# Decode attention on one core: keys loaded one pair ahead of values, and the loads of the first and the last pairs cut differently

## The chip, the cores and the metric

One core of one Trainium2 chip runs the kernel. The metric is the time of one execution in device microseconds, as a median of several runs. Engines, as the profile names them: PE multiplies matrices (PEld is the loading of its stationary operand), DVE is the vector engine, ACT the scalar engine, POOL the GpSimd engine, SP the engine that issues nearly all loads. An engine works through its own instructions in order; engines wait for each other through semaphores.

## The reference

```python
B, Hq, Hkv, Sq, Sk, D = 1, 32, 8, 1, 65536, 128      # q, k, v in bfloat16
rep = Hq // Hkv
k = jnp.repeat(k, rep, axis=1)
v = jnp.repeat(v, rep, axis=1)
scale = D ** -0.5
scores = jnp.einsum("bhqd,bhkd->bhqk", q, k) * scale
p = _softmax(scores, axis=-1)
return jnp.einsum("bhqk,bhkd->bhqd", p, v)
```

One new token attends to 65,536 cached positions. Four query heads share each of eight key and value heads. Keys and values are 134.2 MB each, 268.4 MB together, and every byte is used once.

## The kernel before

The sequence of one key head is cut into four chunks of 128 x 128 positions. Two chunks are a *pair*, so a head has two pairs and the program 16 (`NP`); a pair's keys are 8.4 MB and its values 8.4 MB. `n` is the chunk in the pair. A chunk is 128 tiles of 128 positions, worked on in 16 units of 8 tiles (`j`).

**Keys.** A unit's eight tiles are transposed by PE against an identity (line 135), copied from PSUM to SBUF by DVE (line 207) or, for j = 3, 7, 11, 15, by ACT (line 205), and then multiplied with the head's four queries (line 144); the scores follow the transposes three units later. **Softmax.** For each chunk DVE takes the maximum (line 225), POOL takes it across partitions (line 393), DVE merges it with the old one, ACT makes the exponentials (line 347) and the factor alpha (line 351) by which DVE rescales the sum and the output so far. **Values.** PE multiplies the 128 exponentials' tiles with the value tiles into PSUM (line 162), and DVE adds the result to `acc` (lines 257, 259, 309). In the last pair the old `acc` goes into the last chunk's accumulation through an fp32 matmul with the identity (line 155).

**Loops.** PE runs a loop over the 16 pairs: keys of both chunks, then values of both chunks. ACT loops over pairs, DVE and POOL over heads with two pairs in the body. SP's code (lines 413 to 448) is written out pair by pair.

**Buffers and loads.** `kbuf` holds a whole pair of keys (two halves), `bbuf` one chunk, `vbuf` a whole pair of values. For pairs 1 to 13 (`WHOLE`) the keys come in one load into `kbuf`; POOL (six copies, line 213) and ACT (two, line 356) copy the second half into `bbuf`, from which PE reads chunk 1. For the other pairs chunk 1 is loaded into `bbuf` directly. SP issues in the order K0 V0 K1 V1 ... K15 V15. Three semaphores hold it: `kfree`, three times a pair (POOL's copies done, ACT's copies done, chunk 0's last transposes done), for the next keys; `bfree` (chunk 1's last transposes done) where `bbuf` is loaded directly; `vfree` (DVE has seen the end of the pair's values) for the next values. A load that is cut into pieces has a semaphore for each piece, which PE awaits at the piece's first tile; where a pair comes whole, SP raises the other pieces' semaphores itself (`tokens`). `K_PIECES` and `V_PIECES` are the sizes of the pieces in tiles; `pieces` are used for pair 0's keys, pair 15's first chunk of keys and pair 15's values.

Of the kernel before, what the change touches and what calls it, by code (L numbers as in the profile page):

```python
# [25 lines left out]
K_PIECES = ((64, 64), (64, 64))  # L26
V_PIECES = ((128,), (73, 38, 13, 4))
# [10 lines left out]
def on_act(j):  # L38
    return j % 4 == 3
# [12 lines left out]
def bass_standalone__gqa_softmax__decode_kernel(nc, q, k, v, out):  # L52
# [32 lines left out]
    cmax = sb("cmax", [P, R], DT.float32)  # L85
# [5 lines left out]
    rsum = sb("rsum", [P, R], DT.float32)  # L91
# [17 lines left out]
    vp = [[sem(f"vp{i}_{p}") for p in range(len(V_PIECES[i]))] for i in range(2)]  # L109

# [6 lines left out]
    acr, l_sem, lws = sem("acr"), sem("l_sem"), sem("lws")  # L117
    xd, xa, xg = sem("xd"), sem("xa"), sem("xg")
# [19 lines left out]
    def pe_scores(pe, n, j):  # L138
        take(pe, eva if on_act(j) else evd)
        if n == 0 and j == 0:  # L140
            take(pe, qrdy)
# [7 lines left out]
    def pe_values(pe, n, lap):  # L149
        vv = vbuf[:, n * T * D:(n + 1) * T * D].rearrange("p (t d) -> p t d", d=D)  # L150
        for t in range(T):
            if n and t == V_PIECES[1][0]:
                with pe.If(lap == NP - 1):
                    pe.wait_ge(acr, H)
                    pe.matmul(pvb[n][:, 0:R], lhsT=identf[:, :], rhs=acc[:, :], start=False, stop=False)  # L155
            if t == 0:
                take(pe, vp[n][0], 16)
                take(pe, exd)
            piece = vp[n][starts(V_PIECES[n]).index(t)] if t and t in starts(V_PIECES[n]) else None
            if piece:  # L160
                pe.wait_ge(piece, 16)
            ins = pe.matmul(pvb[n][:, 0:R], lhsT=vv[:, t, :], rhs=pts[n][:, t * R:(t + 1) * R],  # L162
                            start=t == 0, stop=t == T - 1)
            if piece:
                pe.sem_inc(piece, -16)
        ins.then_inc(pvd, 1)

    def pe_pair(pe, lap):
# [9 lines left out]
        for n in range(2):  # L178
            pe_values(pe, n, lap)

    def tensor_engine(pe):
# [6 lines left out]
        with pe.Fori(0, NP) as lap:  # L188
            pe_pair(pe, lap)
        pe.wait_ge(t_f, H)  # L190
# [33 lines left out]
    def chunk_max(e, n):  # L224
        e.tensor_reduce(cmax[:, :], qkb[n][:, :].rearrange("p (t g) -> p g t", g=R),  # L225
                        AX.X, ALU.max).then_inc(cm, 1)

    def new_max(e, n, fresh):
        take(e, cma)

        mn, mo = m[n], m[1 - n]
# [30 lines left out]
    def dve_pair(e, second, lap):  # L262

        fresh, last = not second, second
        for j in range(G):
            if not on_act(j):
                evict(e, 0, j)
# [218 lines left out]
```

## Time and profile before

| what | us |
|---|---|
| median of 3 runs | 628.18 (628.08 to 628.23) |
| span of the profiled execution, first to last instruction | 626.94 |
| what lies around it (median less span) | 1.24 |

No time of the profiled execution itself is listed beside its span; the median of the runs stands for it. In timelines a row gives start, duration, engine, line, operation and the tiles written and read; brackets give the idle time of the engine before it and what ended it. `SPq` rows are loads issued by SP. "issue" as a releaser means that the profile shows nothing that the engine waited for. In the list of loads the last number is the time from issue to landing.

### The profile page before, as it was taken

Reading aid. Unit: us, or ns where it says so; the run is one execution under the profiler, and the core shown is the slowest. Engines: PE = TensorE matmul, PEld = TensorE weight load, DVE = VectorE, ACT = ScalarE, POOL = GpSimd, SP = SyncE. Lnnn points to the kernel's source line nnn. Section 1 sums busy time; section 2 is a strip of 40 time slices with the busy share of each in tenths; the row PEclk is TensorE's granted clock in tenths of the full one; section 3 lists DMA queues with packets and bytes.
Section 4 is the critical chain, followed back from the end, with each engine's and each line's share of the span. In section 5 each row is a group of like instructions: output and inputs, shape, how many; then the busy total and the mean of one; then the engine's idle time right before and its main releaser. Section 6 shows DMA issues by size and latency. Waiting matters only on the chain. (4 is left out here: it accounts for less than half of the span.)

```text
span 626.9 us, 27931 instructions
## 1 busy us (share of the span) xinstructions
PE 484.6 (77%) x12340; PEld 478.9 (76%) x12340; DVE 315.1 (50%) x699; ACT 228.9 (37%) x445; POOL 159.9 (26%) x124
## 2 busy tenths in 40 slices
PE   5752995959859498694976959679496894999698
PEld 5752995949859498694976959679496894999698
DVE  4620752817537174371734717356183562848274
ACT  2320532615335153341634407245062441624133
POOL 0000704307042070520605115060150702400000
PEclk9965875958769587695966959678596785969597
DMA  8999999999999999999999999999999999999997
GB/s 366 440 449 424 439 431 439 431 439 426 443 422 447 410 460 410 460 406 460 410 439 431 426 443 426 443 426 439 431 439 431 439 431 435 416 447 424 420 433 302
DMA packets 6280, 268.57 MB, mean 428 GB/s; under 512 B 896, under 2 KB 1024, under 8 KB 1152
## 3 DMA queue, kind: packets, MB, share of 16 engines
q1 hardware_dynamic: 6224, 268.45, 99.2%
q8 instruction: 6, 0.10, 0.1%
q10 hardware_dynamic: 48, 0.01, 0.0%
q14 instruction: 2, 0.02, 0.0%
HBM read 268.44 MB, written 0.01 MB: 428 GB/s over the span
## 5 line engine op out<-in xcount | busy, mean ns | idle before, releaser
L207 DVE COPY ktb<-trb 128x1024 bf16<-128x1024 bf16 x384 | 254.6, 689 | 177.5 <-PE trb L135 173.7
L205 ACT ACTIVATE ktb<-trb 128x1024 bf16<-128x1024 bf16 x128 | 131.0, 1023 | 352.7 <-PE trb L135 297.9
L135 PE MATMUL trb<-ident,kbuf 128*128 128x128 bf16 x2048 | 177.1, 245 | 104.7 <-PEq L49 104.6
L135 PEld LDWEIGHTS trb<-ident,kbuf 128*128 128x128 bf16 x2048 | 143.9, 111 | 105.6 <-issue 105.5
L213 POOL COPY bbuf<-kbuf 128x2048 bf16<-128x2048 bf16 x78 | 143.9, 1893 | 177.6 <-POOLq L49 177.6
L144 PE MATMUL qkb<-qcur,ktb 128*128 128x4 bf16 x4096 | 174.3, 165 | 11.8 <-PEq L49 10.3
L144 PEld LDWEIGHTS qkb<-qcur,ktb 128*128 128x128 bf16 x4096 | 155.2, 97 | 14.6 <-issue 14.6
L135 PE MATMUL trb<-ident,bbuf 128*128 128x128 bf16 x2048 | 157.0, 220 | 5.2 <-issue 3.9
L162 PE MATMUL pvb<-pts,vbuf 128*128 128x4 bf16 x4096 | 113.0, 166 | 15.2 <-PEq L49 11.0
L162 PEld LDWEIGHTS pvb<-pts,vbuf 128*128 128x128 bf16 x4096 | 111.1, 103 | 16.6 <-issue 15.6
L135 PEld LDWEIGHTS trb<-ident,bbuf 128*128 128x128 bf16 x2048 | 117.4, 97 | 5.5 <-issue 5.5
L393 POOL PARTITION_ALL_REDUCE cmaxa<-cmax x32 | 11.9, 370 | 254.1 <-POOLq L49 254.1
L347 ACT ACTIVATE pts<-qkb,negm 128x128 bf16<-128x128 f32 x128 | 50.9, 549 | 37.2 <-ACTq L49 37.2
L356 ACT ACTIVATE bbuf<-kbuf 128x2048 bf16<-128x2048 bf16 x26 | 49.5, 1902 | 0.0
L347 ACT ACTIVATION_READ_ACCUMULATOR pts<-qkb,negm 128x1 f32 x128 | 35.6, 278 | 0.0
L225 DVE TENSOR_REDUCE cmax<-qkb 128x4 f32<-128x512 f32 x32 | 22.0, 686 | 23.4 <-DVEq L49 23.4
L259 DVE TENSOR_TENSOR acc<-acc,pvb 128x4 f32<-128x4 f32 x16 | 2.5, 158 | 30.0 <-PE pvb L162 30.0
L257 DVE COPY acc<-pvb 128x4 f32<-128x4 f32 x8 | 1.3, 163 | 21.8 <-PE pvb L162 21.8
L395 POOL PARTITION_ALL_REDUCE la<-lp x8 | 3.4, 430 | 30.7 <-POOLq L49 30.7
L236 DVE SCALAR_TENSOR_TENSOR negm<-cmaxa,m 128x4 f32<-128x4 f32 x24 | 3.9, 163 | 11.7 <-DVEq L49 11.5
L351 ACT ACTIVATE alpha<-dm 128x4 f32<-128x4 f32 x32 | 7.1, 221 | 0.0
L250 DVE TENSOR_TENSOR acc<-acc,alpha 128x4 f32<-128x4 f32 x24 | 3.9, 164 | 6.1 <-DVEq L49 5.7
(44 smaller groups left out, 41.6 us busy)
## 6 DMA issues: line engine op xcount, KB each, us to landing
kbuf<-in_k_dram SPq DMA_DIRECT2D x4, 2048.0 KB, 16.3
bbuf<-in_k_dram SPq DMA_DIRECT2D x2, 4096.0 KB, 20.9
bbuf<-in_k_dram SPq DMA_DIRECT2D x2, 2048.0 KB, 19.9
kbuf<-in_k_dram SPq DMA_DIRECT2D x1, 4096.0 KB, 16.3
vbuf<-in_v_dram SPq DMA_DIRECT2D x1, 4096.0 KB, 21.9
vbuf<-in_v_dram SPq DMA_DIRECT2D x1, 2336.0 KB, 27.1
vbuf<-in_v_dram SPq DMA_DIRECT2D x1, 1216.0 KB, 29.6
vbuf<-in_v_dram SPq DMA_DIRECT2D x1, 416.0 KB, 30.1
```

The source lines that it names most:

```text
L135: ins = pe.transpose(trb[j % NTB][:, i * P:(i + 1) * P], kv[:, t, :], ident[:, :])
L144: ins = pe.matmul(qkb[n][:, t * R:(t + 1) * R], lhsT=ktb[:, off:off + P], rhs=qcur[:, :], start=True, stop=True)
L162: ins = pe.matmul(pvb[n][:, 0:R], lhsT=vv[:, t, :], rhs=pts[n][:, t * R:(t + 1) * R], start=t == 0, stop=t == T - 1)
L205: e.activation(dst, trb[j % NTB][:, :], AF.Copy).then_inc(eva, 1)
L207: e.tensor_copy(dst, trb[j % NTB][:, :]).then_inc(evd, 1)
L213: ins = op(bbuf[:, c * CB * D:(c + 1) * CB * D], kbuf[:, off:off + CB * D])
L225: e.tensor_reduce(cmax[:, :], qkb[n][:, :].rearrange("p (t g) -> p g t", g=R), AX.X, ALU.max).then_inc(cm, 1)
L236: return e.scalar_tensor_tensor(to[:, :], cmaxa[:, :], -scale, mo[:, :], ALU.mult, ALU.min)
L347: ins = e.activation(pv[:, g, :], sv[:, g, :], AF.Exp, bias=negm[:, g:g + 1], scale=scale, accum_out=rsum[:, g:g + 1])
L351: e.activation(alpha[:, :], dm[:, :], AF.Exp, scale=1.0).then_inc(sx, 1)
L356: return e.activation(o, i, AF.Copy)
L393: e.partition_all_reduce(cmaxa[:, :], cmax[:, :], P, bass.bass_isa.ReduceOp.max).then_inc(cma, 1)
```

## The change

- SP's order becomes K0 K1 V0 K2 V1 ... K15 V14 V15. `keys(p)` issues a pair's keys, for pairs 1 to 13 also waits for `bfree`, and `values(p - 1)` follows it.
- PE's loop has 17 laps: lap p does the keys of pair p, then the values of pair p - 1; the first lap skips the values and the last one the keys, by branches on the lap.
- The softmax step is done once for a pair instead of once for a chunk: both maxima and their maximum on DVE, one reduction on POOL, eight exponentials in a row and one alpha on ACT.
- The values of both chunks go into one PSUM accumulation, which starts with the fp32 identity matmul of `acc`; `acc` is zero for a head's first pair and the rescaled PSUM result for its second. DVE finishes a head's output in the next pair.
- Exponentials now wait until the previous pair's values have used their buffer (`pfree`), and PE's scores wait until the previous pair's exponentials have read the scores (`exd`).
- Pair 14's values come in two loads. Pair 15's values follow into the same buffer half by half: the first half when pair 14's first half has been used (`vhalf`, raised by ACT), the second after `vfree`.
- Pieces: chunk 0's keys of pairs 0 and 15 in 32, 40 and 56 tiles, their chunk 1 in one; the last chunk of values in 73, 33, 15 and 7.

```diff
-K_PIECES = ((64, 64), (64, 64))
-V_PIECES = ((128,), (73, 38, 13, 4))
+K_PIECES = ((32, 40, 56), (128,))
+V_PIECES = ((128,), (73, 33, 15, 7))
...
     def pe_scores(pe, n, j):
         take(pe, eva if on_act(j) else evd)
-        if n == 0 and j == 0:
-            take(pe, qrdy)
+        if j == 0:
+            take(pe, exd)
+            if n == 0:
+                take(pe, qrdy)
...
+    def pe_values(pe, lap):
+        take(pe, acr)
+        pe.matmul(pvb[0][:, 0:R], lhsT=identf[:, :], rhs=acc[:, :], start=True, stop=False)
+        for n in range(2):
+            vv = vbuf[:, n * T * D:(n + 1) * T * D].rearrange("p (t d) -> p t d", d=D)
+            sems = dict(zip(starts(V_PIECES[n]), vp[n]))
+            for t in range(T):
+                piece = sems.get(t)
+                if piece:
+                    pe.wait_ge(piece, 16)
+                ins = pe.matmul(pvb[0][:, 0:R], lhsT=vv[:, t, :], rhs=pts[n][:, t * R:(t + 1) * R],
+                                start=False, stop=n == 1 and t == T - 1)
+                if piece:
+                    pe.sem_inc(piece, -16)
+            ins.then_inc(pvd if n else pfree, 1)
...
-        with pe.Fori(0, NP) as lap:
-            pe_pair(pe, lap)
-        pe.wait_ge(t_f, H)
+        with pe.Fori(0, NP + 1) as lap:
+            with pe.If(lap < NP):
+                pe_keys(pe)
+            with pe.Else():
+                pe.wait_ge(exd, 2)
+            with pe.If(lap > 0):
+                pe_values(pe, lap)
+        pe.wait_ge(t_f, 1)
...
+    def pair_max(e):
+        for n in range(2):
+            take(e, qkd)
+            ins = e.tensor_reduce(cmax[:, n * R:(n + 1) * R], qkb[n][:, :].rearrange("p (t g) -> p g t", g=R),
+                                  AX.X, ALU.max)
+        own(e, ins, xd)
+        e.tensor_tensor(cmaxp[:, :], cmax[:, 0:R], cmax[:, R:2 * R], ALU.max).then_inc(cm, 1)
...
+        for n in range(2):
+            for j in range(G):
+                if not on_act(j):
+                    evict(e, n, j)
+                if n == 0 and j == 0:
+                    e.sem_inc(pgo, 1)
+        pair_max(e)
+        if second:
             next_queries(e)
         else:
             e.sem_inc(qrdy, 1)
-        values_done(e, 0, fresh)
-        rescale(e, 1, False)
...
+        new_max(e, second)
+        if second:
+            values_done(e)
+        else:
+            with e.If(lap > 0):
+                values_done(e)
+                own(e, e.tensor_tensor(oT[:, HR - R:HR], pvb[0][:, 0:R], recip[:, :], ALU.mult), xd)
...
+        take(e, sx)
+        if not second:
+            e.memset(acc[:, :], 0.0).then_inc(acr, 1)
...
+        e.tensor_tensor(acc[:, :], pvb[0][:, 0:R], alpha[:, :], ALU.mult).then_inc(acr, 1)
...
-        for j in (3, 7):
+        for j in (3, 7, 11, 15):
             evict(e, 1, j)
-        exps(e, 0)
-        for j in (11, 15):
-            evict(e, 1, j)
-        exps(e, 1)
+        for n in range(2):
+            take(e, pfree)
+            if n == 0:
+                e.sem_inc(vhalf, 1)
+            exps(e, n)
+        take(e, dmr)
+        e.activation(alpha[:, :], dm[:, :], AF.Exp, scale=1.0).then_inc(sx, 1)
...
+        def keys(p):
             if p:
                 e.wait_ge(kfree, 3 * p)
             if WHOLE[0] <= p < WHOLE[1]:
-                e.dma_start(kbuf[:, :], ks).then_inc(kp[0][0], 16)
+                e.dma_start(kbuf[:, :], src(kf, p)).then_inc(kp[0][0], 16)
                 tokens(kp[0][1:])
...
+                e.wait_ge(bfree, p)
+                tokens(kp[1])
+                return
+            key_unit(p, 0)
             if p:
+                e.wait_ge(bfree, p)
+            key_unit(p, 1)
...
+        def values(p):
+            vs = src(vf, p)
+            if p < NP - 2:
+                if p:
+                    e.wait_ge(vfree, p)
                 e.dma_start(vbuf[:, :], vs).then_inc(vp[0][0], 16)
...
+            for n in range(2):
+                if p == NP - 2:
+                    if not n:
+                        e.wait_ge(vfree, p)
+                    e.dma_start(half(vbuf, n), half(vs, n)).then_inc(vp[n][0], 16)
+                    tokens(vp[n][1:])
+                else:
+                    e.wait_ge(vfree if n else vhalf, p + 1 - n)
+                    pieces(half(vbuf, n), half(vs, n), V_PIECES[n], vp[n])
+
+        for p in range(NP):
+            keys(p)
+            if p:
+                values(p - 1)
+        values(NP - 1)
```

165 lines of the change are left out of this document (48 added, 117 removed).

## The prediction

> **What bounds the kernel now.** I read the page first, then the chain of waits, the loads with their issues, and the timeline of three stretches: pair 0, a steady pair, the tail.
>
> ```profile
> span 626.9 us, 27931 instructions
> PE 484.6 (77%) x12340; PEld 478.9 (76%) x12340; DVE 315.1 (50%) x699; ACT 228.9 (37%) x445; POOL 159.9 (26%) x124
> q1 hardware_dynamic: 6224, 268.45, 99.2%
> q8 instruction: 6, 0.10, 0.1%
> ```
>
> SP's queue keeps the 16 DMA engines busy for 99.2% of the span; the busiest compute engine has 77%. So the time is that of one unbroken stream of loads, plus a lead-in and a tail. An engine made faster is worth nothing; a load issued after its predecessor has drained costs exactly its lateness.
>
> ```profile
> 63.08 3.50 PE L135 MATMUL trb<-ident,kbuf 128*128 128x128 bf16 x32 [9.04 <-PEq L49]
> 64.40 11.07 POOL L213 COPY bbuf<-kbuf 128x2048 bf16<-128x2048 bf16 x6 [25.25 <-POOLq L49]
> ...
> 75.70 0.33 SPq L418 DMA_DIRECT2D kbuf<-in_k_dram  x1
> 333.99 3.57 PE L135 MATMUL trb<-ident,kbuf 128*128 128x128 bf16 x32 [7.96 <-PEq L49]
> 335.43 11.07 POOL L213 COPY bbuf<-kbuf 128x2048 bf16<-128x2048 bf16 x6 [10.83 <-POOLq L49]
> 346.73 0.33 SPq L418 DMA_DIRECT2D kbuf<-in_k_dram  x1
> 358.12 3.45 PE L162 MATMUL pvb<-pts,vbuf 128*128 128x4 bf16 x128
> 358.30 0.69 DVE L225 TENSOR_REDUCE cmax<-qkb 128x4 f32<-128x512 f32 x1 [1.37 <-DVEq L49]
> 361.38 0.21 ACT L351 ACTIVATE alpha<-dm 128x4 f32<-128x4 f32 x1
> 361.74 3.55 PE L162 MATMUL pvb<-pts,vbuf 128*128 128x4 bf16 x128 [0.17 <-PEq L49]
> ...
> 365.51 0.33 SPq L437 DMA_DIRECT2D vbuf<-in_v_dram  x1
> ```
>
> PE starts a pair when its keys land, after 8 to 9 us of idling. From pair 1 (63.08) to pair 8 (333.99) are 7 pairs in 270.91 us: 38.70 us a pair, 19.35 us for each 8.4 MB load. The keys of pair 1 are the third load in the row, so pair 0's keys had landed at 63.0 - 2 x 19.35 = 24.3. In a pair the next keys are issued 12.7 us after PE's start (333.99 to 346.73, set by POOL's copies), the values' matmuls begin at +24.1, and the next values are issued at +31.5.
>
> ```profile
> 592.83 2.23 SPq L407 DMA_DIRECT2D vbuf<-in_v_dram  x5
> 625.77 0.25 SPq L448 DMA_DIRECT2D out_dram<-lrow  x1
> vbuf<-in_v_dram SPq DMA_DIRECT2D x1, 4096.0 KB, 21.9
> vbuf<-in_v_dram SPq DMA_DIRECT2D x1, 2336.0 KB, 27.1
> vbuf<-in_v_dram SPq DMA_DIRECT2D x1, 128.0 KB, 29.9
> 620.83 0.04 issue
> 620.88 2.08 PE pvb L162 x73
> 622.96 0.43 PE pvb L155 x2
> 623.39 1.59 PE pvb L162 x55
> 625.00 0.17 DVE oT L305
> ```
>
> The five last loads are issued 0.45 us apart, so the 128 KB piece goes out at 594.6 and lands at 594.6 + 29.9 = 624.5. PE's last 130 instructions run back to back to 624.98: in the tail PE and the stream end together, within 0.5 us. The 1.96 us after that are output.
>
> **The change part by part.** *The stream.* Bytes stay. Loads go from 42 to 44: pair 0's keys stay four (3+1 for 2+2), pair 15's go from three to four, pair 14's values from one to two, pair 15's values stay five. The price of one more load: 2336 KB landed 5.6 us after the 4096 KB (592.83 + 21.9 = 614.7; 593.3 + 27.1 = 620.4, rounded by 0.1), where 2.39 MB at 8.39 MB per 19.35 us are 5.5. I take 0.08 each; two are **+0.15 us** (0 to 0.4).
>
> *The tail.* The fp32 matmul of the old accumulator (0.43) moves from the middle of the last 128 matmuls to their head, where PE waits for data. PE no longer has the keys and all values of the last load's time to do: after the last landing it has 7 matmuls left instead of 4, 3 x 0.029 = 0.09 us (29 ns from 55 in 1.59). Against PE's 0.5 us after the landing now, I take **-0.05** (-0.3 to +0.3).
>
> *DVE, ACT, POOL.* 16 maxima across partitions, alphas and rescalings disappear, 16 small combinations appear, all 0.16 to 0.4 us; PE gets 15 more fp32 matmul pairs, 0.43 each. In a pair this is +24.1 + 0.43 + 7.2 (358.12 to 365.29) = +31.9, and 6.8 us of the 38.7 stay idle. Cover: the stream. **0.**
>
> *The issues* are where it can lose. A wait on SP holds every later load, as SP issues all of them in order. A small DMA takes 625.77 to the span's end, 1.2 us, so I let every issue need 1.2 us before the queue runs dry:
>
> ```profile
> 8.18 3.57 PE L135 MATMUL trb<-ident,kbuf 128*128 128x128 bf16 x32 [2.94 <-PEq L49]
> 18.91 0.61 PE L135 MATMUL trb<-ident,kbuf 128*128 128x128 bf16 x8
> 19.68 0.33 SPq L418 DMA_DIRECT2D kbuf<-in_k_dram  x1
> 22.75 0.21 PEld L144 LDWEIGHTS qkb<-qcur,ktb 128*128 128x128 bf16 x6 [0.62 <-issue]
> 31.69 0.23 PEld L135 LDWEIGHTS trb<-ident,bbuf 128*128 128x128 bf16 x4 [4.04 <-issue]
> 37.40 0.34 PE L144 MATMUL qkb<-qcur,ktb 128*128 128x4 bf16 x8 [0.78 <-PEq L49]
> 51.02 2.93 PEld L162 LDWEIGHTS pvb<-pts,vbuf 128*128 128x128 bf16 x107 [3.11 <-issue]
> 605.28 0.61 PE L135 MATMUL trb<-ident,bbuf 128*128 128x128 bf16 x8 [1.36 <-PEq L49]
> 617.25 3.44 PE L162 MATMUL pvb<-pts,vbuf 128*128 128x4 bf16 x128
> ```
>
> - Keys of pair 1 now follow pair 0's directly, so they must be out by 24.3 - 1.2 = 23.1. Before, 64 tiles landed at 8.1 and the last transposes ended at 19.52. With 32 tiles first PE starts 32 x 0.076 = 2.4 us earlier, meets the third piece at 13.0, and ends near 17.6: issue at 17.8, cover 5 us.
> - Values of pair 0 wait for bfree, the last transposes of pair 0. Its second half is one piece now and lands at 24.3; 12.0 us of work (605.28 to 617.25), 1.5 for the slow start after idling (32 transposes in 3.57 where eight take 0.61), and 2 to 4 for the stop at 31.69. Keys end at E0 = 40 to 42, transposes 1.7 earlier; issued by 40.5, needed by 43.6 - 1.2. Cover 2 us.
> - Keys of pair 2 go out 12.6 us after pair 1's start (63.08 to 75.70); needed by 63.0 - 1.2 = 61.8. So pair 1 may start as late as 49.2, instead of 43.7. Keys' end to alpha's end is 3.5 us now (358.1 to 361.6); with the second maximum (0.7), the combining (0.3) and four more exponentials (1.4) it is 5.9, and only then DVE evicts again (1.0 us after a start, 63.1 to POOL's 64.4 less 0.3): start in effect at E0 + 4.9 = 45 to 47. Cover 2 to 4 us.
> - In steady pairs: keys 19.35 - 12.7 - 1.2 = 5.4 us of cover, values 38.7 - 32.1 - 1.2 = 5.4.
> - First half of pair 15's values waits until values 14, first half, are done. From the landing of the last keys: 12.0 + 0.43 + 3.45 + 0.3 for ACT and SP + 1.2 = 17.4, against 19.4 us that pair 14's values take. Cover 2 us. The second half: landing + 3.5 + 0.3 + 1.2 = 5.0 into the 9.7 us of the first.
>
> Everywhere there is cover, so the sum is 0.15 - 0.05 + 0 = **+0.1**: 627.0 of span. The runs lie 628.18 - 626.94 = 1.24 above the profiled span, so **628.3 us**.
>
> **The rivals.** *Code not yet loaded.* PE halted at 27.6 to 31.69 and at 47.9 to 51.02 for no semaphore, in lap 0 alone, and the page has just six instruction packets: PE runs into code still being fetched behind the loads. Now lap 0 ends with a jump over the 256 value matmuls (512 instructions with their weight loads), which have never run, to the loop's end. From the stop at 22.75, the first moment to ask for the code that came at 31.69, are 8.9 us; 3.1 is the shortest of the two long stops. So the jump costs 3.1 to 8.9, and pair 1 starts at E0 + 3 to 9 = 43.7 to 51. Past 49.2 the keys of pair 2 are late by the excess, 0 to 1.8 us; with a second fetch behind the first (the values' own code is asked for at the same time) 2 to 4. Price 2: **630.3**. For it: two stops seen in straight code. Against: no halt shows at the loop's back edge, and the jump's first 5 us lie under the wait for keys. The Trainium skill, page "Runtime: NRT & Kernel Launch", section "Instruction fetch mechanics", says that a taken branch to a block outside the loaded window forces a fetch of the target before execution continues; the two stops agree with fetching by blocks, and no trace here shows such a jump.
>
> *All the code again.* If that jump also throws out what was loaded, lap 1 stops at each of six blocks, 3 to 4 us each: keys 2 and values 1 late by 10 to 15 us, **640**. Against it: laps 1 to 15 of before never refetch.
>
> *The turn at pair 15.* If PE goes through keys 15 and values 14 at the slow pace (3.57 for 32 against 0.61 for eight, 1.46 times), the 12.0 become up to 17.5 and the first half goes out 3 us late: **631**. Against: the same stretch in before ran at 0.61 throughout.
>
> *A shorter end.* If the PE backlog held the end more than the 0.5 us that I read, or the lead-in shortens with the smaller first piece, at most 1.5 us: **627**. Against: pieces had landed at 624.5.
>
> **How the numbers follow.** Forecast 0.48, late keys of pair 2 0.32, the turn 0.07, all code again 0.07, shorter end 0.06. A difference under 0.2% (1.26 us) cannot be told from none: 629.4 and 626.9 are the limits. Of the late keys three quarters pass 629.4 (0.24), with the turn and the code 0.38 slower; shorter end gives 0.05 faster; 0.57 remains. The likeliest case's own range is 627.9 to 628.8. To leave out 0.2, the range goes down to 627.6 (tail at its lower bound, half the shorter end) and up to 632.0 (late keys with the second fetch; the turn).
>
> **What would show it.** Right: SP's queue at 99%, PE's wait at pair 1 within 43.7 to 49, the issue of pair 2's keys before 61.8, the last first-half issue of values 2 us before pair 14's values end, PE's end waiting for pieces. Wrong: DMA slices under 9 around 60 to 65 us (late keys), many more instruction packets (code again), a dip near 600 (the turn).

## The result and the profile after

The changed kernel takes **631.96 us** (median of 6 runs, 629.19 to 634.87) against 628.23 (628.08 to 628.33) measured beside it: a ratio of 1.0061, 95% interval 1.0039 to 1.0083. It is slower, by 3.7 us, and its runs scatter over 5.7 us where those of before scatter over 0.25. The forecast was 628.3; the time lies in the range, at its upper end.

The profiled run is one of 631.01 us with a span of 629.5, so 1.5 lie around it, 0.3 more than before; it is 0.95 us under the median. Its page:

```profile
span 629.5 us, 27800 instructions
...
DMA  9999999999999999999999999999999999999997
...
q1 hardware_dynamic: 6512, 268.45, 99.1%
q8 instruction: 6, 0.10, 0.1%
```

SP's queue is still the bound, at 99.1%, and no digit of the DMA row but the last is under 9: slices of 15.7 us are too wide to show a gap of 2. As many instruction packets run as before, so code is not fetched again. The timeline of PE at the turn from pair 0 to pair 1, and at pair 2 (start, duration, instructions; in brackets the idle time before and what ended it):

```profile
38.68 0.34 PE L149 MATMUL qkb<-qcur,ktb 128*128 128x4 bf16 x8 [0.68 <-PEq L49]
47.37 3.30 PE L138 MATMUL trb<-ident,kbuf 128*128 128x128 bf16 x32 [8.35 <-PEq L49]
...
84.47 3.51 PE L138 MATMUL trb<-ident,kbuf 128*128 128x128 bf16 x32 [6.46 <-PEq L49]
```

The one branch over the values' code, grouped by its source line (shortest, median and longest of 17 executions in ns, first and last start):

```profile
L193 PEldq COMPARE_BRANCH  x17: 76/76/7600, 39.0 to 613.0; - x17
```

In lap 0 the branch takes 7.60 us, in the others 0.08. It is the jump over code that has never run: from 39.0 to 46.6 PE's sequencer does nothing else. The Trainium skill, page "Runtime: NRT & Kernel Launch", section "Instruction fetch mechanics", has a taken branch outside the loaded window wait for a fetch; the 7.60 us agree with that. What follows from it stands in SP's issues and in the windows of the DMA share (after the busy times of PE, PEld, DVE, ACT and POOL, each with its count, come the granted clock, the share of the 16 engines and GB/s; a packet counts where it begins, so a full window can show more than 1):

```profile
37.54 0.33 SPq L433 DMA_DIRECT2D vbuf<-in_v_dram  x1
60.00 0.33 SPq L416 DMA_DIRECT2D kbuf<-in_k_dram  x1
78.19 0.33 SPq L433 DMA_DIRECT2D vbuf<-in_v_dram  x1
```

```profile
60.00:62.00 2.00, 2.00 (x57) 2.00 (x54) 1.44 (x3) 0.61 (x1) 0.00 (x0) 1.00 1.04 360
62.00:64.00 2.00, 2.00 (x57) 2.00 (x54) 1.97 (x3) 0.44 (x2) 0.00 (x0) 1.00 0.52 197
64.00:66.00 2.00, 2.00 (x55) 2.00 (x52) 1.40 (x4) 1.00 (x1) 0.00 (x0) 1.00 1.09 459
```

The keys of pair 2 are issued at 60.00, 12.6 us after PE's start at 47.37, as costed. In the window from 62 to 64 only half as many packets begin as the engines could take: the queue ran dry. To size it I read the trace's landing records (when the last of the 16 engines reports its share of a load): a load of 8.4 MB lands 19.35 us after the one before it as long as the queue is full, so what a period has over 19.35 (9.72 for half a load) is lost. Pair 0's values land at 63.03 and pair 2's keys at 84.33, 21.30 later: **1.95 us lost**. The other periods up to pair 14 are 19.35, most within 0.02 (one of 19.45 is followed by one of 19.26); only those of pair 1's keys (19.60) and pair 0's values (19.44) are longer for good, while instruction blocks pass through the same engines. The last piece lands at 627.03 instead of 624.56, 2.47 later: 1.95 from the hole and 0.5 from the lead-in and the smaller loads of pairs 14 and 15.

I call *lead* the time from an issue to the landing of the load in flight (here 63.03 - 60.00 = 3.03 us). The second thin place is at the end:

```profile
604.06 8.85 SPq L395 DMA_DIRECT2D vbuf<-in_v_dram  x5
```

```profile
578.00:584.00 6.00, 6.00 (x136) 6.00 (x134) 5.17 (x9) 2.05 (x2) 0.00 (x0) 0.89 1.00 431
...
604.00:606.00 2.00, 0.00 (x0) 0.00 (x0) 0.00 (x0) 1.59 (x8) 0.00 (x0) 0.50 0.97 311
606.00:608.00 2.00, 0.71 (x24) 0.71 (x25) 0.00 (x0) 0.00 (x0) 0.00 (x0) 0.50 0.65 279
```

Pair 15's first half of values goes out at 604.06 with 3.19 us of lead (pair 14 lands at 607.25). The share sinks to 0.65, but the landings keep their 9.72: the engines that ran ahead idled, the slowest did not (the 16 engines end pair 14 between 604.48 and 607.25).

### The profile page after: what moved, and what is told of

It reads as the page before. It is cut to its first block, busy times and chain, and to the rows that moved or that the text cites. A ratio compares the mean times of both kernels' runs of the same rounds, so it can differ in the third digit from the quotient of the medians.

```text
span 629.5 us, 27800 instructions
## 1 busy us (share of the span) xinstructions
PE 490.4 (78%) x12370; PEld 484.9 (77%) x12370; DVE 303.0 (48%) x601; ACT 230.5 (37%) x429; POOL 154.0 (24%) x108
## 3 DMA queue, kind: packets, MB, share of 16 engines
q1 hardware_dynamic: 6512, 268.45, 99.1%
## 5 line engine op out<-in xcount | busy, mean ns | idle before, releaser
L381 POOL PARTITION_ALL_REDUCE cmaxa<-cmaxp x16 | 5.9, 371 | 261.8 <-POOLq L49 261.8
L288 DVE TENSOR_TENSOR acc<-pvb,alpha 128x4 f32<-128x4 f32 x8 | 1.3, 162 | 58.4 <-DVEq L49 58.4
L279 DVE TENSOR_TENSOR oT<-pvb,recip 128x4 bf16<-128x4 f32 x7 | 1.1, 163 | 38.2 <-DVEq L258 38.2
L156 PE MATMUL pvb<-acc,identf 128*128 128x4 f32 x32 | 6.7, 280 | 4.9 <-PEq L49 4.9
L156 PEld LDWEIGHTS pvb<-acc,identf 128*128 128x128 f32 x32 | 5.8, 226 | 5.9 <-issue 5.9
L322 DVE TENSOR_TENSOR oT<-pvb,recip 128x4 bf16<-128x4 f32 x1 | 0.2, 162 | 12.7 <-PE pvb L164 12.7
## 6 DMA issues: line engine op xcount, KB each, us to landing
vbuf<-in_v_dram SPq DMA_DIRECT2D x1, 1056.0 KB, 13.6
```

The source lines that it names most:

```text
L156: pe.matmul(pvb[0][:, 0:R], lhsT=identf[:, :], rhs=acc[:, :], start=True, stop=False)
L381: e.partition_all_reduce(cmaxa[:, :], cmaxp[:, :], P, bass.bass_isa.ReduceOp.max).then_inc(cma, 1)
```

## The experiments

Theory A: the jump makes PE late for pair 1, so the keys of pair 2 are issued to a queue that is nearly dry. Rivals (theory B in the expectations): the pieces or the order of the loads cost by themselves; the fetching of instructions costs by itself; the turn at pair 15. Times are medians with the range of the runs; ratios are to the kernel before on the same chip.

**1. The changed kernel again, and the pieces alone.** The first without an edit; the second is the kernel before with

```diff
-K_PIECES = ((64, 64), (64, 64))
-V_PIECES = ((128,), (73, 38, 13, 4))
+K_PIECES = ((32, 40, 56), (128,))
+V_PIECES = ((128,), (73, 33, 15, 7))
```

> The changed kernel once more, for its scatter and a second trace. Theory A (PE's jump over the values' code, which is not loaded in lap 0, holds PE; pair 1 starts late, the keys of pair 2 are issued when the queue has run dry): the branch at line 193 has a maximum of 6 to 12 us, PE starts pair 1 at 46 to 51, DMA has a hole of 1 to 6 us around 60 to 66, and the time is 628.5 plus the hole, 629 to 635 over the runs. Theory B (the new order of the loads or the turn at pair 15 costs the time, whatever PE does in lap 0): the hole or the loss is in every run in the same place with nearly the same size, within 0.5 us, and does not follow the branch.

> The kernel before with the changed sizes of the pieces and nothing else (first keys in 32, 40, 56 and 128 tiles, last values 73, 33, 15, 7); no code is jumped over and the loads stay in their old order. Theory A (the jump makes PE late for pair 1, so the keys of pair 2 are issued to a queue that is nearly dry): 628.0 to 628.6, no change. Theory B (the pieces cost by themselves, by a later end of pair 0's keys or by more work behind the last landing): 629 to 632, with a later end of pair 0 or of the last values.

Measured: again 632.08 (630.15 to 635.08), ratio 1.0068 [1.0045, 1.0092], with a branch of 7.94 us and the keys of pair 2 at 60.14. The pieces alone: 628.36 (628.25 to 629.61), 1.0005 [0.9996, 1.0014]. In the old order the pieces cost nothing that can be told. The six runs of the first lie in two groups, 630.2 to 630.6 and 633.6 to 635.1.

**2. The second chunk of the first keys cut in two**, so that pair 0 ends earlier:

```diff
-K_PIECES = ((32, 40, 56), (128,))
+K_PIECES = ((32, 40, 56), (64, 64))
```

> Chunk 1 of the first and last keys in two pieces of 64 tiles again, all else as changed. PE can begin chunk 1 at 19 instead of 24.3, so the keys of pair 0 end at 33 to 35 and the jump begins 4 to 6 us earlier. Theory A: the branch still takes 6 to 9 us but ends by 43.6 or soon after; pair 1 starts at 43.7 to 44.5, the keys of pair 2 are issued at 56.3 to 57.2, no hole; 628.3 to 628.9 with a scatter under 0.5. Theory B: order of loads and pair 15 unchanged, so 630 to 633 and the same scatter.

Measured: 629.62 (628.51 to 630.88), 1.0024 [1.0013, 1.0035]. The branch, PE's start of pair 1 and SP's issue, in the profile of the run of 628.51:

```profile
L193 PEldq COMPARE_BRANCH  x17: 76/76/6099, 37.8 to 610.9; - x17
```

```profile
44.75 3.57 PE L138 MATMUL trb<-ident,kbuf 128*128 128x128 bf16 x32 [6.85 <-PEq L49]
```

```profile
57.38 0.33 SPq L416 DMA_DIRECT2D kbuf<-in_k_dram  x1
```

PE starts pair 1 at 44.75, and the keys of pair 2 have 5.5 us of lead (pair 0's values land at 62.91): no hole, every period behind them 19.35, and 0.3 us above before, although the jump is still there with 6.1 us. In this run the jump by itself costs no more than 0.3, as no issue in its wake is late, and neither does the order of the loads, which is that of the changed kernel. But the run is the fastest of the seven, and its branch is 1.5 us shorter than in the changed kernel, which the edit does not explain; see 8.

**3. Values in front in PE's loop.** The jump then falls in the first lap, before the first keys.

```diff
-        with pe.Fori(0, NP + 1) as lap:
+        with pe.Fori(0, NP + 2) as lap:
+            with pe.If(lap > 1):
+                pe_values(pe, lap)
             with pe.If(lap < NP):
...
-            with pe.If(lap > 0):
-                pe_values(pe, lap)
```

> PE's loop has the values' code ahead of the keys' code (18 laps, values of pair lap - 2), so PE does the same matmuls in the same order and the jump over unloaded code comes at the start of lap 0 near 5 us, before the first keys. Theory A: one long branch of 2 to 5 us near 5 us, none near 39; pair 1 starts at 43.7, the keys of pair 2 are issued by 57; 628.3 to 629.0 (the first keys start 1 to 4 us later, which may make the keys of pair 1 late by up to 1). Theory B: 630 to 633 as changed.

Measured: 635.62 (635.21 to 636.1), 1.0119 [1.0105, 1.0134]. The branch takes 5.89 us at 4.3, the first keys end later, and SP's issues are:

```profile
26.07 0.33 SPq L416 DMA_DIRECT2D kbuf<-in_k_dram  x1
...
62.17 0.33 SPq L416 DMA_DIRECT2D kbuf<-in_k_dram  x1
```

The keys of pair 1 go out at 26.07, after the queue has run dry near 24. The expected 628.3 to 629.0 is missed: the loss has moved from pair 2 to pair 1 and grown, to 6.01 us for an issue 2.02 us after the queue had run dry.

**4. A hint for the branch**, given at the second chunk's first transposes, so that the target is fetched ahead:

```diff
+                if n and j == 0:
+                    loc = pe.mark_branch_hint_location()
...
-            with pe.If(lap > 0):
+            pe.br_lt(lap, 1, on_true="past_values", on_false="do_values").branch_hint(loc)
```

> As changed, with a branch prefetch hint for the jump over the values, placed ahead of chunk 1 of the keys, some 14 us before the jump in lap 0. Theory A: the branch takes under 1 us, PE starts pair 1 at 43.7, the keys of pair 2 are issued at 56.4, no hole; 628.3 to 628.8. If the hint does nothing the branch keeps its 6 to 9 us and the time its 629 to 635. Theory B: the branch becomes short and the time stays at 630 to 633.

Measured: 636.99 (635.43 to 638.8), 1.0148 [1.0134, 1.0163]. The branch, then PE's weight loads in lap 1:

```profile
L196 PEldq COMPARE_BRANCH  x17: 80/84/4764, 39.0 to 617.4; - x17
```

```profile
75.25 3.47 PEld L164 LDWEIGHTS pvb<-pts,vbuf 128*128 128x128 bf16 x127 [5.99 <-issue]
82.30 3.06 PEld L164 LDWEIGHTS pvb<-pts,vbuf 128*128 128x128 bf16 x112 [3.59 <-issue]
```

The jump shrinks to 4.8 us, the keys of pair 2 go out at 57.21 and the hole at 62 is gone, as theory A has it. But the values' code, no longer fetched on the way, now stops PE in lap 1 for 6.0 and 3.6 us, and pair 1's values go out at 85.63, 3.41 us behind the end of the load before, and 5.71 are lost. So the time misses what theory A expected of a working hint.

**5. No jump at all**: the first pair's keys written out ahead of the loop; the second kernel adds 28 fp32 matmuls behind them, the third is the first with the cut of 2.

```diff
-        with pe.Fori(0, NP + 1) as lap:
-            with pe.If(lap < NP):
+        pe_keys(pe)
+        with pe.Fori(0, NP) as lap:
+            with pe.If(lap < NP - 1):
                 pe_keys(pe)
...
-            with pe.If(lap > 0):
-                pe_values(pe, lap)
+            pe_values(pe, lap)
```

> The changed kernel with the first pair's keys written out ahead of PE's loop; the loop is then keys of the next pair, values of this one, and lap 0 jumps over nothing long. Four more blocks of instructions are fetched in all. Theory A: PE halts only for straight code (3 to 4.5 us at most each), pair 1 starts at 43 to 46, the keys of pair 2 are issued by 58.5, there is no hole at 60 to 64, and the time is 628.3 to 629.8 (up to 1.5 for two fetches on one DMA engine). Theory B (the order keys-in-front or the pieces cost, whatever PE's code does): 631 to 633 as the changed kernel.

> The kernel without the long jump, with 28 more fp32 matmuls of 0.43 us (12 us in all, into an unused buffer) between the first pair's keys and the second's: PE's lateness without any jump. Theory A: pair 1 starts at about 51, the keys of pair 2 are issued at about 63.6, the queue is dry for 3 to 5 us around 61 to 66, and the time is 3.5 to 6 us above the kernel without the long jump. If only the jump or its fetches cost, and not the late issue: within 1 us of it.

> No long jump, and the second half of the first keys in two pieces of 64 tiles as in the kernel before. Theory A: the keys of pair 2 are issued by 57, no hole, 628.0 to 629.0, as before or at most 0.8 above, and steadier than the version with the jump and that cut (628.5 to 630.9). If the scatter of that version comes from something else than the late issue (two instruction fetches on one DMA engine, for one), it stays: 628.5 to 631.

Measured: 687.96 (660.65 to 704.37), 643.71 (642.88 to 645.34; 1.0252 [1.0239, 1.0265]) and 696.84 (664.67 to 699.71). All three are far above what was expected. How many instruction blocks each fetched (the rows of the three pages):

```profile
q8 instruction: 47, 0.77, 0.5%
```

```profile
q8 instruction: 11, 0.18, 0.1%
```

```profile
q8 instruction: 58, 0.95, 0.6%
```

The first and the third, with the longer program, fetch code again in some laps, 47 and 58 blocks instead of 6, each time with late issues; none of the theories had this. So "no jump" could not be tried in this way. The second fetches 11 blocks, the last at 93 us; what it shows is lateness without a long jump (SP's issues, then the windows):

```profile
64.51 0.33 SPq L418 DMA_DIRECT2D kbuf<-in_k_dram  x1
93.71 0.33 SPq L435 DMA_DIRECT2D vbuf<-in_v_dram  x1
```

```profile
60.00:62.00 2.00, 1.25 (x28) 1.02 (x24) 1.76 (x3) 1.01 (x1) 2.00 (x2) 1.00 0.04 8
62.00:64.00 2.00, 0.63 (x10) 0.63 (x11) 0.00 (x0) 0.00 (x0) 1.04 (x1) 0.90 0.00 0
```

PE starts pair 1 at 50.64, the keys of pair 2 go out at 64.51, 1.53 us after the load before them has landed, and hardly a packet begins for 4 us: 5.56 are lost. Pair 1's values, behind two more stops of PE (3.73 and 3.54 us, no releaser), go out 5.83 us too late and lose 8.29. The two make 13.9 of the 14.2 us by which the last piece is later than before.

**6. The price of a late issue by itself.** The kernel before, four of its key issues held until PE has reached certain scores (`late` is raised by PE at units 0, 2, 4 and 6 of chunk 1):

```diff
+LATE = (0, 2, 4, 6)
+LATE_PAIRS = {4: 0, 6: 1, 8: 2, 10: 3}
...
+        if n and j in LATE:
+            ins.then_inc(late[LATE.index(j)], 1)
...
+            if p in LATE_PAIRS:
+                e.wait_ge(late[LATE_PAIRS[p]], p)
```

> The kernel before, with four of its key issues made late on purpose: the keys of pairs 4, 6, 8 and 10 wait in addition for PE's scores of groups 0, 2, 4 and 6 of the second half, about 15, 16.4, 17.7 and 19 us after PE's start of the pair instead of 12.7; the queue runs dry at 19.35, so the leads are about 4.2, 2.9, 1.6 and 0.4 us. By the prediction's rule (1.2 us of lead are enough): only the last costs, 0.9 us, 629.1 in all, and the periods of the other three stay 38.70. If a queue needs some 4 us of lead to be refilled without loss: 0, 1.1, 2.4 and 3.6 us, 634 to 636 in all, with the hole growing from one to the next.

Measured: 632.68 (631.73 to 633.62), 1.007 [1.0055, 1.0084]. SP's four issues, and windows behind the last two:

```profile
154.85 0.33 SPq L425 DMA_DIRECT2D kbuf<-in_k_dram  x1
...
233.95 0.33 SPq L425 DMA_DIRECT2D kbuf<-in_k_dram  x1
...
314.43 0.33 SPq L425 DMA_DIRECT2D kbuf<-in_k_dram  x1
...
393.88 0.33 SPq L425 DMA_DIRECT2D kbuf<-in_k_dram  x1
```

```profile
313.00:315.00 2.00, 2.00 (x55) 2.00 (x53) 1.88 (x4) 1.19 (x2) 0.00 (x0) 1.00 0.00 0
...
393.00:395.00 2.00, 2.00 (x56) 2.00 (x53) 1.99 (x3) 1.94 (x11) 0.00 (x0) 1.00 0.69 229
```

With the landings before them (159.45, 236.83, 315.88, 394.31) the leads are 4.60, 2.88, 1.45 and 0.43 us; lost are **0, 1.53, 1.03 and 2.18**. The prediction's rule, 1.2 us of lead are enough, would have had 0, 0, 0 and 0.8. The rule of 4 us has the threshold right, but the loss does not grow in step with the lateness. From 313 to 315 no packet of data begins. By the trace's packets the first of the load issued at 314.43 begin at 315.4, 1.0 us later, and take 3.0 to 3.3 us instead of 2.42; the engines are up to 2 us apart, so those that are ahead are idle long before the last one is.

**7. The jump at the start of the program.** The values in front, and PE's warm-up inside the loop behind them, so that the jump falls where PE waits anyway; the second with the cut of 2.

```diff
+        with pe.Fori(0, NP + 2) as lap:
+            with pe.If(lap > 1):
+                pe_values(pe, lap)
+            with pe.If(lap < 1):
+                pe.wait_ge(t_id, 1)
...
+            with pe.If(lap < NP):
+                pe_keys(pe)
```

> The changed kernel with the values' code at the head of PE's loop and PE's warm-up inside the loop behind it: the jump over the not yet loaded values' code falls at 0 us, while PE has nothing to do until 4 us, and no code is added. Theory A (the time of the long jump is what costs): the keys of pair 1 are issued by 20, the keys of pair 2 by 58.5, no hole at either place, 628.2 to 629.8. If the jump at 0 us is not hidden (the stop lasts to 8 us or more, or further stops follow in the first keys as in the version with values in front): 631 to 636. If the order of the loads itself costs: 631 or more without any late issue of keys.

> The jump at 0 us, and the second half of the first keys in two pieces of 64 tiles. Theory A: all issues have more lead, 628.0 to 629.0, as before, and the scatter of 2.4 us that the version with the cut alone showed is gone. If that scatter comes from something else (instruction fetches that meet on one DMA engine), it stays, 628.5 to 631.

Measured: 633.07 (630.7 to 634.28), 1.0071 [1.0058, 1.0083]; 632.73 (631.0 to 633.95), 1.0073 [1.006, 1.0086]. A miss: the jump is not hidden. PE, then SP, in the first kernel's profile:

```profile
6.17 1.34 PE L188 MATMUL pvb<-ident 128*4 128x4 bf16 x48 [6.17 <-issue]
```

```profile
22.48 0.33 SPq L417 DMA_DIRECT2D kbuf<-in_k_dram  x1
...
58.33 0.33 SPq L417 DMA_DIRECT2D kbuf<-in_k_dram  x1
...
604.90 7.82 SPq L396 DMA_DIRECT2D vbuf<-in_v_dram  x5
```

PE's first matmul comes at 6.17 (3.26 in the changed kernel), the keys of pair 1 go out with 1.44 us of lead and lose 2.28; the keys of pair 2, now with 6.6 us (58.33 to 64.90), lose nothing. The other late issue in this profile is pair 15's first half of values: 2.20 us of lead, **2.84 lost**. That is the turn at pair 15. PE's windows at the first keys of that pair, to set beside 0.89 in the changed kernel:

```profile
578.00:584.00 6.00, 6.00 (x108) 5.80 (x107) 4.22 (x9) 1.92 (x5) 0.00 (x0) 0.70 1.01 437
```

The granted clock was 0.70 there, and the first half went out 17.2 us after the landing before it (587.68) instead of 16.2 (587.83). In the second kernel the keys of pair 1 have 1.42 us of lead and lose 2.31.

**8. The turn taken away.** Pair 15's first half of values in two loads; the first waits only for the first 64 tiles of pair 14's. Once with the late keys left in, once with the cut of 2.

```diff
-V_PIECES = ((128,), (73, 33, 15, 7))
+V_PIECES = ((64, 64), (73, 33, 15, 7))
...
+                if n == 0 and t == 63:
+                    ins.then_inc(vquart, 1)
...
+                    for i, s in enumerate((vquart, vhalf)):
+                        e.wait_ge(s, p if i == 0 else p + 1)
+                        o = i * 64 * D
+                        e.dma_start(vbuf[:, o:o + 64 * D], vs[:, o:o + 64 * D]).then_inc(vp[0][i], 16)
```

> The changed kernel with the first half of pair 15's values in two loads of 64 tiles; the first goes out when PE has done the first 64 tiles of pair 14's values, some 1.8 us earlier than the whole half did. The jump and the late keys of pair 2 stay. If there are two late issues (the keys of pair 2, about 2 us in every run, and the turn at pair 15, 0 to 3 us from run to run): 629.8 to 631, with less scatter than the changed kernel's 629.2 to 635. If the jump alone costs and its length makes the scatter: 632 median and the same scatter as the changed kernel.

> Both: the second half of the first keys in two pieces of 64 tiles (which took away the late keys of pair 2) and pair 15's first half of values in two loads. If these are the two late issues and all that costs: 628.2 to 628.8, and the runs lie within 0.6 us, as in the kernel before. If the scatter of the version with the cut alone (628.5 to 630.9) has another cause: 629 to 630 with that scatter still there.

Measured: 630.86 (four runs at 630.06 to 631.03, two at 633.07 and 633.56), 1.0055 [1.0039, 1.0071]; 630.69 (628.91 to 631.01), 1.0031 [1.0021, 1.0041]. In the first the quarter goes out at 601.71 with 4.9 us of lead and the periods at pair 15 are exact, yet two runs at 633 remain, neither of them profiled: the turn is hardly what makes them. The keys of pair 2 are late as before (lead 3.03, lost 1.01). The second missed its 628.2 to 628.8; its branch was the longest of the kernels with the cut so far:

```profile
L195 PEldq COMPARE_BRANCH  x17: 76/76/8159, 38.3 to 613.0; - x17
```

8.16 us in the same place where 2 had 6.10; so the keys of pair 2 went out at 59.94, lead 3.03, and lost 1.89. The cut does not take the late keys away by itself; it needs a short jump, and the same code of PE has a jump of 6.0 or 6.1 us in one run and of 8.2 or 8.8 in another (here, in 2 and in 10). In the five profiles of the changed kernel it is always 7.5 to 7.9. From the trace's packets: the instruction packet that ends the jump runs at 41.4 in the profile of 2 and at 43.8 to 44.0 in those of the changed kernel and of this one, 2.4 us apart, which is what one 64 KB packet of the loads takes.

**9. Three more profiles of the changed kernel**, to catch one of its long runs. No edit.

> The changed kernel once more, one profile, to catch one of its long runs (its runs lie near 630.5 or near 633.5). If the length of the jump makes the difference, a run near 633.5 has a branch of about 10 us in place of 7.6 to 7.9, pair 1 starts at about 50, and the keys of pair 2 are issued at about 62.5 with a period of 24 us behind them. If the turn at pair 15 makes it, the branch is 7.6 to 8 us and the period of pair 15's first half is 2 to 3 us long instead.

> As for the first of these three looks: near 630.5 with a branch of 7.6 to 8 us, or near 633.5 with either a branch of about 10 us or a long period at pair 15.

> As for the first of these three looks: near 630.5 with a branch of 7.6 to 8 us, or near 633.5 with either a branch of about 10 us or a long period at pair 15.

Measured: 634.15, 630.66 and 631.27. The long one, first the branch, then PE, SP, and the windows:

```profile
L193 PEldq COMPARE_BRANCH  x17: 76/76/7760, 42.6 to 614.9; - x17
```

```profile
33.86 0.27 PE L138 MATMUL trb<-ident,bbuf 128*128 128x128 bf16 x2
36.47 0.49 PE L138 MATMUL trb<-ident,bbuf 128*128 128x128 bf16 x6 [2.34 <-issue]
...
42.27 0.34 PE L149 MATMUL qkb<-qcur,ktb 128*128 128x4 bf16 x8 [0.78 <-PEq L49]
```

```profile
41.12 0.33 SPq L433 DMA_DIRECT2D vbuf<-in_v_dram  x1
63.85 0.33 SPq L416 DMA_DIRECT2D kbuf<-in_k_dram  x1
...
606.06 8.71 SPq L395 DMA_DIRECT2D vbuf<-in_v_dram  x5
```

```profile
38.00:40.00 2.00, 2.00 (x34) 2.00 (x31) 1.38 (x2) 0.03 (x1) 0.00 (x0) 0.50 1.13 492
40.00:42.00 2.00, 1.49 (x42) 1.40 (x39) 1.29 (x2) 0.90 (x1) 0.00 (x0) 0.89 0.28 107
...
62.00:64.00 2.00, 2.00 (x56) 2.00 (x53) 1.17 (x3) 1.02 (x1) 1.62 (x1) 1.00 0.08 33
```

The jump has its usual length, but begins at 42.6 instead of 39.0. Before it PE stopped 2.34 us in straight code of the second chunk (0.42 at this place in the first profile), and went on at half the granted clock (0.50 from 38 to 40, where it was 1.00). So the *values of pair 0*, which wait for the last transposes, went out at 41.12 instead of 37.54: lead 2.43, lost 2.73. The keys of pair 2 followed at 63.85 and lost 0.85, pair 1's values 0.43, the turn at pair 15 (lead 3.10) 1.00: together 5.0 of the 5.55 us by which the last piece is later than before. Neither expected cause of the long runs was the first; it is a third late issue, and the others come behind it.

The other two have branches of 7.52 and 7.68 us. In both the keys of pair 2 are late (leads 3.13 and 3.02, lost 1.83 and 1.00), and in the one of 631.27 the turn loses 1.02 too. So the keys of pair 2 lost something in all five profiles of the changed kernel, 0.85 to 1.95, and the turn in two of the five.

**10. More lead for the keys by another means**: five copies on POOL and three on ACT, in the second kernel of 8 and in the kernel of 2.

```diff
-POOL_COPIES = (0, 1, 2, 3, 4, 5)
-ACT_COPIES = {3: (6,), 7: (7,)}
+POOL_COPIES = (0, 1, 2, 3, 4)
+ACT_COPIES = {3: (5, 6), 7: (7,)}
```

> The version with the cut and the quarters, and with five of the eight copies of a key pair on POOL and three on ACT (6 and 2 before): POOL's part ends 1.85 us earlier, so every issue of keys comes about 1.8 us earlier in its pair. The jump stays, with its 6 to 8 us. Theory A (late issues are all that costs; a lead of 4.6 us costs nothing): the keys of pair 2 are issued at about 58.1 even behind a long jump, no loss there, 628.2 to 628.8, all runs within 0.6 us. If the jump or its fetches cost by themselves: 629 to 631 as the version without the third copy on ACT.

> The version with the cut alone, with the same three copies on ACT; the last values' first half stays in one load. Theory A with the turn costing nothing in most runs: 628.2 to 629.0. If the turn at pair 15 still costs in some runs: a median as the other's, with single runs 1 to 3 us above it.

Measured: 632.05 (628.97 to 633.78), 1.006 [1.0041, 1.008]; 632.19 (630.74 to 635.45), 1.0075 [1.0058, 1.0092]. A miss: the issue comes 13.6 us after PE's start, not 10.8. POOL, then ACT, in the first kernel:

```profile
45.95 9.24 POOL L220 COPY bbuf<-kbuf 128x2048 bf16<-128x2048 bf16 x5 [5.93 <-POOLq L49]
```

```profile
49.15 3.70 ACT L342 ACTIVATE bbuf<-kbuf 128x2048 bf16<-128x2048 bf16 x2
...
58.27 1.02 ACT L212 ACTIVATE ktb<-trb 128x1024 bf16<-128x1024 bf16 x1 [1.14 <-ACTq L49]
```

POOL ends at 55.2, but ACT, with two copies in a row, comes late to its evictions, PE waits for them, and `kfree` is completed by chunk 0's last transposes, at whose eviction (58.27) SP issues (58.23). In the changed kernel the last transposes ended at 58.77, 1.0 us ahead of POOL (59.77), so that shortening POOL's part could give no more than 1 us of the expected 1.8. What the profile of the first does show: its run had a jump of 6.0 us, the keys of pair 2 had 4.89 us of lead, all periods from there on are 19.35, and it took 629.09; four of its six runs took 631.6 to 633.8 and were not profiled. In the second's the branch took 8.76, the lead was 1.95, and 1.16 us were lost there, 0.59 more at the turn.

The leads and losses of these profiles (without the first and third kernel of 5), worked out from SP's issues and the landing records. "Last begin" is from the trace's packets: how long after the issue the last DMA engine that had run dry begins its first packet of the new load ("none": no engine had run dry).

```
late issue (where)                       lead us   last begin   lost us
keys of pair 2 (10, first)                 4.89      2.99        0
values of pair 1 (8, first)                4.72      3.48        0.16
values of pair 1 (9, run of 631)           4.68      3.19        0.08
quarter of pair 15 (10, first)             4.63      none        0
keys of pair 4 (6)                         4.60      2.58        0
values of pair 1 (9, long run)             3.80      3.62        0.43
first half, pair 15 (7, second)            3.31      2.03        0.18
first half, pair 15 (2)                    3.24      1.65        0
first half, pair 15 (changed kernel)       3.19      1.59        0
first half, pair 15 (1, changed kernel)    3.18      1.33        0
first half, pair 15 (9, run of 631)        3.15      3.00        1.02
first half, pair 15 (4)                    3.14      none        0
keys of pair 2 (9, run of 630)             3.13      3.60        1.83
first half, pair 15 (9, long run)          3.10      3.01        1.00
keys of pair 2 (changed kernel)            3.03      3.84        1.95
keys of pair 2 (8, first)                  3.03      2.71        1.01
keys of pair 2 (8, second)                 3.03      3.45        1.89
keys of pair 2 (9, run of 631)             3.02      2.89        1.00
keys of pair 2 (1, changed kernel)         3.01      3.81        1.54
values of pair 1 (10, second)              3.01      1.99        0
first half, pair 15 (5, second)            2.92      none        0
keys of pair 6 (6)                         2.88      3.33        1.53
first half, pair 15 (9, run of 630)        2.74      1.97        0
values of pair 0 (9, long run)             2.43      3.42        2.73
first half, pair 15 (7, first)             2.20      3.58        2.84
keys of pair 2 (10, second)                1.95      2.15        1.16
first half, pair 15 (3)                    1.89      1.69        0.46
first half, pair 15 (10, second)           1.83      2.02        0.59
keys of pair 2 (9, long run)               1.79      1.65        0.85
keys of pair 8 (6)                         1.45      1.69        1.03
keys of pair 1 (7, first)                  1.44      1.72        2.28
keys of pair 1 (7, second)                 1.42      1.81        2.31
keys of pair 10 (6)                        0.43      1.74        2.18
keys of pair 2 (5, second)                -1.53      1.70        5.56
keys of pair 1 (3)                        -2.02      1.92        6.01
values of pair 1 (4)                      -3.41      1.66        5.71
values of pair 1 (5, second)              -5.83      1.69        8.29
```

At 4.6 us of lead and over no more than 0.16 us is lost, as much as some periods with 7 us of lead show in the first profile of 8 (19.52). At 3.8 and under, 0 to 2.8 us are lost, and not in step with the lead. At leads of 2.7 to 3.4 the loss goes with the last begin: where no dry engine begins later than 2.03 us after the issue, 0 to 0.18; where one begins 2.7 to 3.0 after it, 1.00 to 1.02; where one begins 3.3 to 3.8 after it, 1.5 to 1.95. Most dry engines begin within 1.0 to 1.7; why a few take longer is not shown. Behind a queue that is dry altogether (the last four rows) 2.3 to 4.0 us are lost on top of the lateness.

## Why the prediction was wrong

- **The step that failed** is "so I let every issue need 1.2 us before the queue runs dry". It was taken from a small DMA's whole time at the end. Measured, 4.6 us are enough and 3.8 are not safe. With it fell "Everywhere there is cover": by the table, the cover was short at the keys of pair 2 and at the turn in the profiled run, and in the long run at pair 0's values too. "A load issued after its predecessor has drained costs exactly its lateness" fell as well: issues 1.5 to 5.8 us late cost 2.3 to 4.0 us more than that.
- **The jump.** Its price, 3.1 to 8.9 us, held: 5.9 to 8.8 without a hint, 7.5 to 7.9 in the changed kernel. Its effect was sized by the failed step: pair 1 started at 47.37, inside the forecast's own "as late as 49.2", and the keys went out before its limit of 61.8, and still 1.95 us were lost. So the rival *late keys of pair 2* was the right one, with a threshold up to 3.4 us too late. That its price (2 us: 630.3) fits the profiled run's hole is luck: it counted the start's lateness past 49.2, and there was none. With 4.6 in place of 1.2 its condition would have been a start past 45.8 instead of 49.2; most of 43.7 to 51 lies past that, and it would have been the likeliest case.
- **Values of pair 0**, "issued by 40.5, needed by 43.6 - 1.2. Cover 2 us". Issued at 37.54 in the first profile and at 41.12 in the long run: past the estimate, but inside the limit of 42.4, and still 2.73 us were lost, so this is the failed step again. The stop of 2.34 us lay within the 2 to 4 that were counted; the clock that halved behind it (eight transposes in 1.01 instead of 0.61) was not counted. This makes the long run caught, and perhaps the group at 633 to 635, of which one profile alone is known.
- **The turn at pair 15.** The sum was right, 17.4 of 19.4 us gone with 1.2 counted in: measured lead 3.19 against 3.2. Its rival wanted PE at the slow pace for the whole stretch and 3 us of delay; no delay was needed. At leads of 2.74 to 3.19 the five profiles of the changed kernel lost 0 three times, 1.00 and 1.02; 1 us more of delay in 7 made it 2.84.
- **The range.** The median of 631.96 lies just under the range's upper end of 632.0. That is luck: the range reached there by a second fetch behind the jump and by the turn at PE's slow pace, three of the six runs lie above it, and the one long run that was profiled got there mostly by pair 0's values.
- **Stream and tail.** +0.15 and -0.05 were costed. In the profiled run the lead-in and the loads of pairs 14 and 15 cost 0.5. In the two profiles that lost nothing at a late issue the last piece came 0.2 and 0.5 later than before, with two and three loads more than the changed kernel (runs of 628.51 and 629.09). The tail held: the last output goes out 1.24 us after the last landing, 1.21 before.
- **All the code again** did not happen in the changed kernel (six instruction packets); the first and third kernels of 5 fetched code again.
- **DVE, ACT, POOL** at 0 held: the keys of a pair are issued 12.6 us after PE's start as before, and every period in the middle of the run is 19.35.
- **Open.** What makes the jump's length change between runs of the same code (6.0 to 8.8 with the cut); why some engines begin a late load 2 us after the others; whether the instruction fetches cost beside delaying issues; why two kernels of 5 fetch their loop again. Of the changed kernel's runs above 632 one alone was profiled, so that late issues make them all is argued, not shown; the same holds for the spread of the versions of 8 and 10. No version measured beat the kernel before.

## What to carry to other kernels

Where one stream of loads sets the time, write down for each issue how long before the queue runs dry it comes, in the first and last laps above all; here an issue with 3.8 us of lead or less cost up to 2.8 us, even where the load in flight had 3 us to go, and one behind a dry queue 2.3 to 4.0 us more than it was late. The loop here skips its body's second half in the first lap, so it jumps over code that isn't there and pays for it at the moment when the pipeline has least slack; moving the jump or hinting it moved the cost to another late issue, and writing the first lap out made code be fetched again in two kernels of three. A median with a scatter of several us beside a steady old one may point to such thresholds, as it did here: take profiles until one of the long runs is among them.

## What the runs showed of the hardware

- A branch over some 512 instructions that have not run took 5.9 to 8.8 us while loads filled the DMA queue, and 0.08 once they had run. With a hint it took 4.76, and the skipped code was fetched later (stops of 5.99 and 3.59).
- The landing records agree with each instruction block of 16 KB going through one of the 16 DMA engines that carry the loads: in the kernel before, the engines end a load within 0.4 us of each other at 13 us (before the first block has passed) and 1.9 us apart at 19 us and from there to the end. In the profile of the changed kernel they are 2.7 to 2.8 apart from pair 2's keys to pair 14.
- A loop of some 1,550 PE instructions stayed loaded over 16 laps as long as little stood before it; with 1,000 instructions of the same code written out ahead of it, 47 and 58 blocks were fetched in a run, in bursts, and the time rose to 660 to 704 us. With those and 28 more matmuls ahead of the loop there were only 11, which is not explained.
- On engines that had run dry the first packets began 1.0 us after the issue and took 3.0 to 3.3 us each instead of 2.42 (6). With a lead of about 3 us a few engines got their first packet only 2.7 to 3.8 us after the issue, and what is lost goes with that (the table behind 10).
